# PV with V as weights for column units, and softmax sums added on Pool and VectorE

## The chip, the core and the metric

The kernel runs on one core of a Trainium2 chip. A core has five engines, each with a queue that is worked off in order: PE (TensorE, the matrix multiplier), DVE (VectorE), ACT (ScalarE), POOL (GpSimd) and SP, which here only issues DMA transfers. They share an on-chip memory (SBUF, 128 partitions); PE writes into PSUM, whose banks hold 128 x 512 fp32 values, and DVE and ACT read results from there. Engines wait for each other by semaphores.

The metric is the device time of one execution in microseconds (us). Before the change it is 1303.84 us, the median of three runs (1303.82 to 1304.23).

## What is computed

One transformer block: adaptive layer norm, attention with 32 query heads over 8 cached key and value heads, and a gated MLP. The change concerns the attention:

```python
q = (x @ wq).reshape(B, Sq, Hq, Dh).transpose(0, 2, 1, 3)   # Sq = 2048, Hq = 32, Dh = 128
k = jnp.repeat(k_cache, 4, axis=1)                          # 8 key heads, Sk = 2048
v = jnp.repeat(v_cache, 4, axis=1)
scores = jnp.einsum('bhqd,bhkd->bhqk', q, k) * Dh ** (-0.5)
p = softmax(scores, axis=-1)
o = jnp.einsum('bhqk,bhkd->bhqd', p, v)
return o.transpose(0, 2, 1, 3).reshape(B, Sq, Hq * Dh) @ wo
```

The kernel takes the exponential P of the scaled scores without subtracting a maximum, multiplies it with V, and divides by the sum of P over the keys at the end. (Another path, not taken here, redoes everything if a sum leaves a safe range.)

## The kernel before

**Units.** The attention is cut into 8 x 16 = 128 units: a unit `u` is one key head g = u // 16 and one tile of 128 queries j = u % 16, with the four query heads (REP = 4) that share the key head. A loop over iterations `it` runs 128 units and six more; each iteration has eight slots (NSLOT = 8). In iteration `it`, `qk(it, i)` makes the scores of unit `it` in slot i, and in the same slot PE works off an eighth of the PV product of an earlier unit, a q projection matmul of a coming unit (`fill`), and a matmul of the projection by wo of a still earlier unit. The program order is written out by hand: what stands in a slot is issued there, and `at(it, slot, fn)` puts a function at the head of a slot, behind those put there earlier.

**Two forms of unit.** The scores can be made with the keys on the partitions or with the queries on them.

- A column unit (L1056 to L1070) makes scores transposed: 128 keys of one key tile on the partitions, 512 columns (four heads of 128 queries), two key tiles to a slot. ACT writes their exponential straight to `pTs[u]`, 16 key tiles of 128 x 512, which is the form that PV needs. Its PV (`pv`, L1106) takes P as the weights and V as the moving operand: 64 matmuls of 129 columns. The 129th column of V is ones, so the sum of P over the keys comes with it. DVE then takes the reciprocal (L1125) and normalises into `onorms[u]` (L1126), a DMA transpose turns this to `oTs[u]` (L1137), and the four matmuls by wo (L1171) are added up in one PSUM bank, which DVE adds to `xaccs[j]` (L1158).
- A row unit (L1017 to L1037) has queries on the partitions and 1024 keys to a slot. ACT sums each row while it takes the exponential (`accum_out`), so the sums cost nothing more than two small DVE operations (L1082, L1085), and a DMA transpose (L1078, one for each head) turns P into `pTs[u]`. Its PV (`pv_rows`, L1087) takes V as the weights and P as the moving operand: 16 matmuls of 512 columns, whose result is already transposed; DVE copies it to `oTs[u]` (L1102). As nothing is normalised yet, each head's wo matmul gets a bank of its own, and DVE scales it by the reciprocal sum while adding (L1164).

From unit 5 to 121 the forms come in threes, row, row, column: `by_rows(u)` tells which. 78 units are row units. Units 7, 10, ..., 109 and 112, 115, 118, 121 are the column units among them. PV of a row unit runs two or three iterations after its scores (`LAGS`), PV of a column unit in the next iteration; wo comes three iterations after PV. So in a period of three iterations, called C, N1 and N2 in the prediction, C makes the scores of a column unit, N1 runs its PV while it makes the scores of a row unit, and N2 is a second row unit.

**What is shared.** The PSUM name `misc` has two banks, used in turn by the q projection (one head in each iteration, four matmuls in slots 0 to 3, copied to `qT` by DVE, L970, at the end of slot 3) and by the wo matmuls (slots 4 to 7). `s_ps` has two double banks for scores, `o_ps` two banks for PV. P lives in three buffers (`homes`). SP's queue carries all row turns, the turns of `onorms`, and the loads of each head group (L721 to L744); for each new v, Pool sets its column of ones first (L727).

**The last head group** (units 112 to 127) is followed by a second layer norm for each query tile: Pool multiplies and adds 128 x 512 values there (L1187, L1188). DVE normalises (`xn2`), and DMA turns it (`xnT2`), in `ln2`.

Of the kernel before, what the change touches and what calls it, by code (L numbers as in the profile page):

```python
# [10 lines left out]
BF16 = mybir.dt.bfloat16  # L11
FP32 = mybir.dt.float32
ACT = mybir.ActivationFunctionType
ALU = mybir.AluOpType
AX = mybir.AxisListType
P = 128
# [559 lines left out]
def kernel(  # L576
# [19 lines left out]
    nc = tc.nc  # L596
    _, S, D = A_x.shape
    _, HKV, SK, DH = A_k_cache.shape
    HQ = A_wq.shape[1] // DH
    REP = HQ // HKV  # L600
# [4 lines left out]
    NT = S // P  # L605
    NDT = D // P
    NKT = SK // P
# [5 lines left out]
    NSLOT = NKT // 2  # L613
# [26 lines left out]
    res = fast.enter_context(tc.tile_pool(name="res", bufs=1))  # L640
    stat = fast.enter_context(tc.tile_pool(name="stat", bufs=2))
# [3 lines left out]
    late = free_b.enter_context(tc.tile_pool(name="late", bufs=2, side="right"))  # L645
# [27 lines left out]
    def bank2():  # L673
        return psum.tile([P, 1024], FP32, name="s_ps")
# [11 lines left out]
    def normalise(dst, src, mv, rstd):  # L686
        nc.vector.tensor_scalar(
            out=dst,
            in0=src,
            scalar1=mv,  # L690
            scalar2=rstd,
            op0=ALU.subtract,
            op1=ALU.mult,
        )
# [287 lines left out]
    def by_rows(u):  # L982
        return TURN_A <= u < TURN_B and (u - TURN_A) % len(LAGS) < len(LAGS) - 1

    row_units = [u for u in range(NU) if by_rows(u)]

    def pv_at(u):
# [15 lines left out]
    def at(it, slot, fn):  # L1003
        later.setdefault((it, slot), []).append(fn)

    def qk(u, i):
        g, j = divmod(u, NT)
        b, jj = g * NCH + j // CT, j % CT
        if i == 0:
            if homes[u] == "wsp":  # L1010
                pTs[u] = wspp.tile([P, NT, 512], BF16, name="wsp")
            else:
                pTs[u] = late.tile([P, NKT, 512], BF16, name=homes[u], bufs=1)
            if by_rows(u):
                rsums[u] = stat.tile([P, NSLOT], FP32, name="rs")
        s_ps = bank2()
        if by_rows(u):  # L1017
            hh, half = divmod(i, 2)
            for c in range(2):
                k0 = (2 * half + c) * 512  # L1020
                nc.tensor.matmul(  # L1021
                    s_ps[:, c * 512 : (c + 1) * 512],
                    lhsT=qTs[b][:, hh, jj * P : (jj + 1) * P],
                    rhs=groups[g]["kT"][:, k0 : k0 + 512],
                    start=True,
                    stop=True,
                )
            nc.scalar.activation(  # L1028
                out=rows_of(u, hh)[:, half * HK : (half + 1) * HK],
                in_=s_ps[:],  # L1030
                func=ACT.Exp,
                scale=inv_sqrt_dh,
                accum_out=rsums[u][:, i : i + 1],
            )
            if half == 1:
                at(*divmod(u * NSLOT + i + 1, NSLOT), lambda: turn_rows(u, hh))
            return  # L1037
        if u < 2:
            pair, k0 = i // 4, i % 4 * 4
            qs = slice(pair * 256, (pair + 1) * 256)  # L1040
            for kt in range(4):
                nc.tensor.matmul(  # L1042
                    s_ps[:, kt * 256 : (kt + 1) * 256].rearrange("p (r q) -> p r q", r=2),
                    lhsT=groups[g]["kT"][:, (k0 + kt) * P : (k0 + kt + 1) * P],
                    rhs=qTs[b][:, 2 * pair : 2 * pair + 2, jj * P : (jj + 1) * P],
                    start=(kt % 2 == 0),
                    stop=(kt % 2 == 1),
                )
            nc.scalar.activation(
                out=pTs[u][:, k0 : k0 + 4, qs],  # L1050
                in_=s_ps[:].rearrange("p (k q) -> p k q", k=4),
                func=ACT.Exp,
                scale=inv_sqrt_dh,
            )
            return
        for h in range(2):  # L1056
            kt = 2 * i + h
            nc.tensor.matmul(  # L1058
                s_ps[:, h * 512 : (h + 1) * 512].rearrange("p (r q) -> p r q", r=REP),
                lhsT=groups[g]["kT"][:, kt * P : (kt + 1) * P],  # L1060
                rhs=qTs[b][:, :, jj * P : (jj + 1) * P],
                start=True,
                stop=True,
            )
        nc.scalar.activation(  # L1065
            out=pTs[u][:, 2 * i : 2 * i + 2, :],
            in_=s_ps[:].rearrange("p (k q) -> p k q", k=2),
            func=ACT.Exp,
            scale=inv_sqrt_dh,
        )  # L1070

    def rows_of(u, hh):
        return pn[(row_units.index(u) * REP + hh) % len(pn)][:, 0:SK]
# [71 lines left out]

    def wo_proj(u):
        g, j = divmod(u, NT)
        each = by_rows(u)
        ps = {}

        def into(first, X_ps, scale):
            if first:
                xaccs[j] = late.tile([P, D], FP32, name=f"xacc{j}", bufs=1)
            xa = xaccs[j]
            if scale is None and first:
                nc.vector.tensor_copy(out=xa[:], in_=X_ps[:])
            elif scale is None:
                nc.vector.tensor_tensor(out=xa[:], in0=X_ps[:], in1=xa[:], op=ALU.add)  # L1158
            elif first:
                nc.vector.tensor_scalar(  # L1160
                    out=xa[:], in0=X_ps[:], scalar1=scale, scalar2=None, op0=ALU.mult
                )
            else:
                nc.vector.scalar_tensor_tensor(  # L1164
                    out=xa[:], in0=X_ps[:], scalar=scale, in1=xa[:], op0=ALU.mult, op1=ALU.add
                )

        def mm(hh):
            if hh == 0 or each:
                ps[0] = bank("misc")  # L1170
            nc.tensor.matmul(  # L1171
                ps[0][:],
                lhsT=oTs[u][:, hh, :],
                rhs=groups[g]["wo"][:, hh, :],
                start=(hh == 0 or each),
                stop=(hh == REP - 1 or each),
            )
            if each:
                c0 = u * REP + hh
                into(g == 0 and hh == 0, ps[0], rall[:, c0 : c0 + 1])  # L1180
            elif hh == REP - 1:
                into(g == 0, ps[0], None)
            if hh < REP - 1 or g < HKV - 1:
                return
            xa = xaccs[j]
            engine = nc.gpsimd if j < NT - CT else nc.vector
            engine.tensor_tensor(out=xa[:], in0=xa[:], in1=ga_rows[:], op=ALU.mult)  # L1187
            engine.tensor_tensor(  # L1188
                out=x_sb[:, j, :], in0=xa[:], in1=x_sb[:, j, :], op=ALU.add
            )  # L1190
            if j >= NT - CT:
                ln_stats(mv2, j, x_sb[:, j, :])

        return [lambda hh=hh: mm(hh) for hh in range(REP)]

    def ln2(it, j):

        st = {}

        def first():  # L1200
            if j < NT - CT:
                ln_stats(mv2, j, x_sb[:, j, :])
            st["rstd"] = rstd_of(mv2[:, j : j + 1, :], 1, "ln2")

        def second():
            xn = res.tile([P, D], BF16, name="xn2", bufs=2)
            normalise(xn[:], x_sb[:, j, :], mv2[:, j, 0:1], st["rstd"][:, 0:1])
            st["xnT"] = res.tile([P, NDT, P], BF16, name="xnT2", bufs=2)
            nc.sync.dma_start_transpose(out=st["xnT"][:], in_=xn[:])

        def third():
            ch, c0 = j // CT, (j % CT) * P
            if ch not in h2Ts:
                h2Ts[ch] = res.tile([P, NDT, 512], BF16, name="hT", bufs=NCH)
            for dt in range(NDT):
                nc.vector.tensor_scalar(
                    out=h2Ts[ch][:, dt, c0 : c0 + P],
                    in0=st["xnT"][:, dt, :],
                    scalar1=modc[:, 4 * NDT + dt : 4 * NDT + dt + 1],
                    scalar2=modc[:, 3 * NDT + dt : 3 * NDT + dt + 1],  # L1220
                    op0=ALU.mult,
                    op1=ALU.add,
                )

        at(it + 1, 0 if j >= NT - CT else 2, first)
        at(it + 1, 4, second)
        at(it + 2, 3, third)

# [43 lines left out]
        first[j] = ln1_stats(j, 1)  # L1272

    def tile_norm(j):
        xn = res.tile([P, D], BF16, name="xn2", bufs=2)
        normalise(xn[:], x_sb[:, j, :], mv1[:, j, 0:1], first[j][:, 0:1])
        first[j] = xn

# [193 lines left out]
        at(NU + 5, 5 + ch, lambda ch=ch: z2_norm(ch))  # L1472

    def pv_part(u, i, n):
        if by_rows(u):
            return pv_rows(u, i, n)
        for k in range(NSLOT // n):
            pv(u, i * (NSLOT // n) + k)
# [250 lines left out]
```

## Time and profile before

| what | value |
|---|---|
| profiled execution | 1303.83 us, of it span 1302.0 us |
| PE busy | 1287.0 us, 99% of the span |
| ACT busy | 1112.8 us, 85% |
| DVE busy | 685.7 us, 53% |
| POOL busy | 59.0 us, 5% |
| queue that carries SP's transfers | its packets take 87.5% of the time of 16 DMA engines |
| matmuls of PV in column form (L1114) | 3200 |
| matmuls of PV in row form (L1093) | 1248 in all (as weight loads of L1093) |
| granted PE clock | full in every slice |

Busy time is the time in which an instruction of the engine runs, by the hardware profiler. PE's matmuls overlap, so the mean duration of one (379 ns for 512 columns) is longer than the distance from one to the next (0.22 us). In a timeline a line gives the start, the duration, the engine, the line of the kernel, the operation, its output and input tiles, and at its end, in brackets, how long the engine had stood idle and what released it. A window's line gives, for each engine, the busy time in the window and the number of instructions that start in it.

### The profile page before, as it was taken

How to read it: one execution, taken by the hardware profiler on the slowest of the kernel's cores; microseconds unless marked ns; L12 is line 12 of the kernel's file. 1: busy time of each engine (PE TensorE's matmuls, PEld its weight loads, DVE VectorE, ACT ScalarE, POOL GpSimd, SP SyncE). 2: the span in 40 equal slices, each digit the busy share in tenths (PEclk: the TensorE clock that was granted, in tenths of full speed). 3: DMA queues.
4: the chain of work that ended last, by engine and by line, in shares of the span. 5: the costliest groups of instructions: out<-in, count | busy, mean ns of one | idle time of the engine just before them, and what ended most of it. 6: DMA issues, size and time to landing. Idle time of an engine off the chain costs nothing.

```text
span 1302.0 us, 22572 instructions
## 1 busy us (share of the span) xinstructions
PE 1287.0 (99%) x8512; PEld 700.2 (54%) x8665; DVE 685.7 (53%) x1777; ACT 1112.8 (85%) x1683; POOL 59.0 (5%) x99
## 2 busy tenths in 40 slices
PE   9999999999999999999999999999999999999998
PEld 7655555555555555555555555555555556644445
DVE  7545455545554555455545554555455566784444
ACT  7999999999999999999999999999999998650000
POOL 2000000000000000000000000000000133410000
PEclk9999999999999999999999999999999999999999
DMA  7999999999999999999999999999999973254300
GB/s 207 183 188 181 168 184 191 190 166 188 189 181 177 186 174 189 183 171 188 190 175 181 187 192 181 169 195 173 176 193 165 172 146 91 49 138 98 81 21 32
DMA packets 774997, 211.18 MB, mean 162 GB/s; under 512 B 759264, under 2 KB 773216, under 8 KB 774880
## 3 DMA queue, kind: packets, MB, share of 16 engines
q1 hardware_dynamic: 772864, 207.94, 87.5%
q10 hardware_dynamic: 2016, 1.71, 0.4%
q8 instruction: 70, 1.15, 0.4%
q14 instruction: 47, 0.39, 0.1%
HBM read 21.37 MB, written 2.10 MB: 18 GB/s over the span
## 4 chain that ended last, share of the span: by engine, by line
PE 98%; issue 1%; ACT 1%; DMA 0%; SPq 0%; DVE 0%; ACTq 0%
PE s_ps L1021 21%; PE o_ps L1093 20%; PE o_ps L1114 14%; PE s_ps L1058 13%; PE misc L1171 8%; PE misc L959 8%; PE misc L1573 7%; PE s_ps L1397 2%; PE s_ps L1436 2%; PE o_ps L1606 1%; PE s_ps L1042 0%; PE s_ps L1606 0%; DMA kT<-in_A_k_cache_dram 0%; ACT pn L1028 0%; ACT win_sb L1028 0%
## 5 line engine op out<-in xcount | busy, mean ns | idle before, releaser
L1021 PE MATMUL s_ps<-kT,qT 128*128 128x512 bf16 x1219 | 365.0, 379 | 2.3
L1028 ACT ACTIVATE win_sb<-s_ps 128x1024 bf16<-128x1024 f32 x312 | 319.0, 1023 | 3.4 <-PE s_ps L1021 0.7
L1093 PE MATMUL o_ps<-pT,v 128*128 128x512 bf16 x909 | 272.6, 379 | 1.5
L1164 DVE SCALAR_TENSOR_TENSOR xacc<-misc,rall,xacc 128x512 f32<-128x512 f32 x304 | 227.5, 748 | 69.2 <-PE misc L1171 61.7
L1058 PE MATMUL s_ps<-qT,kT 128*128 128x512 bf16 x768 | 228.4, 379 | 0.8
L1065 ACT ACTIVATE pT<-s_ps 128x1024 bf16<-128x1024 f32 x208 | 209.8, 1024 | 11.8 <-PE s_ps L1058 3.6
L1028 ACT ACTIVATE pn<-s_ps 128x1024 bf16<-128x1024 f32 x208 | 212.7, 1023 | 2.3 <-PE s_ps L1021 0.7
L1093 PEld LDWEIGHTS <-v 128*128 128x128 bf16 x1248 | 121.9, 98 | 147.9 <-issue 1.1
L1065 ACT ACTIVATE wsp<-s_ps 128x1024 bf16<-128x1024 f32 x176 | 179.8, 1023 | 12.4 <-PE s_ps L1058 4.6
L1171 PE MATMUL misc<-wo_g,oT 128*128 128x512 bf16 x479 | 181.6, 379 | 1.0
L1021 PEld LDWEIGHTS <-qT 128*128 128x128 bf16 x1248 | 121.4, 98 | 109.4 <-issue 0.4
L959 PE MATMUL misc<-hT,wq_g 128*128 128x512 bf16 (+1 forms) x499 | 178.3, 369 | 0.5
L970 DVE CAST qT<-misc 128x512 bf16<-128x512 f32 x126 | 86.5, 687 | 153.5 <-PE misc L959 153.5
L1114 PEld LDWEIGHTS <-pT 128*128 128x128 bf16 x1792 | 119.6, 98 | 48.8
L1082 DVE TENSOR_TENSOR tot<-rs 128x1 f32<-128x1 f32 x312 | 48.4, 155 | 171.3 <-ACT win_sb L1028 114.9
L1114 PE MATMUL o_ps<-v,pT 128*128 128x129 bf16 x1792 | 137.5, 220 | 0.6
L1058 PEld LDWEIGHTS <-kT 128*128 128x128 bf16 x768 | 74.1, 98 | 81.1 <-issue 1.1
L1114 PEld LDWEIGHTS <-wsp 128*128 128x128 bf16 x1408 | 94.3, 98 | 41.5
L1114 PE MATMUL o_ps<-v,wsp 128*128 128x129 bf16 x1408 | 108.5, 220 | 0.5
L1028 ACT ACTIVATE wmod_a<-s_ps 128x1024 bf16<-128x1024 f32 x104 | 106.3, 1023 | 0.6 <-PE s_ps L1021 0.4
L1573 PE MATMUL misc<-wsp,z 128*128 128x512 bf16 (+2 forms) x554 | 100.1, 336 | 0.3
L1093 PE MATMUL o_ps<-wsp,v 128*128 128x512 bf16 x292 | 87.8, 379 | 0.4
(118 smaller groups left out, 894.6 us busy)
## 6 DMA issues: line engine op xcount, KB each, us to landing
wo_g<-in_A_wo_dram SPq DMA_DIRECT2D x8, 512.0 KB, 4.5
wq_g<-in_A_wq_dram SPq DMA_DIRECT2D x7, 512.0 KB, 4.1
v<-in_A_v_cache_dram SPq DMA_DIRECT2D x7, 512.0 KB, 4.7
wsp<-in_w_mod_dram SPq DMA_DIRECT2D x1, 2048.0 KB, 9.1
pT<-win_sb SPq DMA_TRANSPOSE x117, 5.0
win_sb<-in_B_w_in_dram SPq DMA_DIRECT2D x1, 1792.0 KB, 7.3
x_sb<-in_A_x_dram SPq DMA_DIRECT2D x3, 512.0 KB, 7.0
out_dram<-yout ACTq DMA_DIRECT2D x12, 128.0 KB, 1.7
```

Source lines behind the costliest of these rows:

```text
L959: nc.tensor.matmul(ps[0][:, o0 : o0 + n], lhsT=wqs[g][:, dt, hh * DH : (hh + 1) * DH], rhs=hTs[ch][:, dt, c0 : c0 + n], start=(dt == 0), s ...
L970: nc.vector.tensor_copy(out=dst, in_=src)
L1021: nc.tensor.matmul(s_ps[:, c * 512 : (c + 1) * 512], lhsT=qTs[b][:, hh, jj * P : (jj + 1) * P], rhs=groups[g]["kT"][:, k0 : k0 + 512], sta ...
L1028: nc.scalar.activation(out=rows_of(u, hh)[:, half * HK : (half + 1) * HK], in_=s_ps[:], func=ACT.Exp, scale=inv_sqrt_dh, accum_out=rsums[u ...
L1058: nc.tensor.matmul(s_ps[:, h * 512 : (h + 1) * 512].rearrange("p (r q) -> p r q", r=REP), lhsT=groups[g]["kT"][:, kt * P : (kt + 1) * P], ...
L1065: nc.scalar.activation(out=pTs[u][:, 2 * i : 2 * i + 2, :], in_=s_ps[:].rearrange("p (k q) -> p k q", k=2), func=ACT.Exp, scale=inv_sqrt_dh,)
L1082: nc.vector.tensor_tensor(out=tot[:], in0=rs[:, 2 * hh : 2 * hh + 1], in1=rs[:, 2 * hh + 1 : 2 * hh + 2], op=ALU.add)
L1093: nc.tensor.matmul(o_pss[u][:], lhsT=groups[g]["v1"][:, kt, 0:DH], rhs=pTs[u][:, kt, :], start=(kt == 0), stop=(kt == NKT - 1),)
L1114: nc.tensor.matmul(o_ps[:, hh % 2, 0 : DH + 1], lhsT=pTs[u][:, kt, hh * P : (hh + 1) * P], rhs=groups[g]["v1"][:, kt, 0 : DH + 1], start=( ...
L1164: nc.vector.scalar_tensor_tensor(out=xa[:], in0=X_ps[:], scalar=scale, in1=xa[:], op0=ALU.mult, op1=ALU.add)
L1171: nc.tensor.matmul(ps[0][:], lhsT=oTs[u][:, hh, :], rhs=groups[g]["wo"][:, hh, :], start=(hh == 0 or each), stop=(hh == REP - 1 or each),)
L1573: nc.tensor.matmul(g_pss[f][:, :n], lhsT=z2[:, st, f * P : (f + 1) * P], rhs=wsp[t][:, st, c0 : c0 + n], start=(st == 0), stop=(st == NT - ...
```

## The change

`by_sums(u)` names the column units among the row units that lie before the last head group: 35 units, 7, 10, ..., 109. They keep their scores (column form), but:

- PV takes V as the weights (`pv_rows`): 16 matmuls of 512 columns instead of 64 of 129. The ones column no longer gives the sums.
- `key_sums(u)` makes the sums. Pool adds key tiles 0 to 11 into an fp32 tile, eleven adds of 128 x 512, put into the slots of iteration u. DVE adds key tiles 12 to 15 into another, three adds, at slots 0, 1 and 2 of iteration u + 1. At slot 4 of u + 1 Pool joins the two into a bf16 tile. This holds, for each of 128 keys modulo the tile, a partial sum for 512 columns. At slot 0 of u + 2 SP issues a DMA transpose that puts queries on the partitions, and at slot 1 of u + 3 DVE sums over the 128 values that are left for each head and takes the reciprocal.
- The wo projection takes the form of a row unit: four banks, four scaled adds.

The fp32 tiles `acc` take the room of `xn2` and `xnT2`; `ln2` uses the two halves of one `acc` tile in their place, and the first tiles' normalisation a half of one.

```diff
+    def by_sums(u):
+        return TURN_A <= u < (HKV - 1) * NT and not by_rows(u)
...
             if by_rows(u):
                 rsums[u] = stat.tile([P, NSLOT], FP32, name="rs")
+            if by_sums(u):
+                key_sums(u)
...
+    N_POOL = 12
+
+    def key_sums(u):
+        acc = [res.tile([P, D], FP32, name="acc", bufs=2) for _ in range(2)]
+        pT = pTs[u]
+
+        def add(engine, a, kt, first):
+            engine.tensor_tensor(
+                out=a[:],
+                in0=pT[:, first, :] if kt == first + 1 else a[:],
+                in1=pT[:, kt, :],
+                op=ALU.add,
+            )
+
+        for kt in range(1, N_POOL):
+            at(*divmod(u * NSLOT + kt // 2 + 1, NSLOT), lambda kt=kt: add(nc.gpsimd, acc[0], kt, 0))
+        for kt, (unit, slot) in zip(range(N_POOL + 1, NKT), ((1, 0), (1, 1), (1, 2))):
+            at(u + unit, slot, lambda kt=kt: add(nc.vector, acc[1], kt, N_POOL))
+
+        def join():
+            onorms[u] = late.tile([P, REP, P], BF16, name="onorm", bufs=3)
+            nc.gpsimd.tensor_tensor(
+                out=onorms[u][:],
+                in0=acc[0][:].rearrange("p (r q) -> p r q", r=REP),
+                in1=acc[1][:].rearrange("p (r q) -> p r q", r=REP),
+                op=ALU.add,
+            )
+
+        turned = {}
+
+        def turn():
+            xn = res.tile([P, D], BF16, name="xn1", bufs=4)
+            turned["t"] = xn[:].rearrange("p (r q) -> p r q", r=REP)
+            nc.sync.dma_start_transpose(
+                out=turned["t"], in_=onorms[u][:].rearrange("p r q -> p (r q)")
+            )
+
+        def close():
+            tot = stat.tile([P, REP], FP32, name="tot4")
+            nc.vector.tensor_reduce(out=tot[:], in_=turned["t"], axis=AX.X, op=ALU.add)
+            nc.vector.reciprocal(out=rall[:, u * REP : (u + 1) * REP], in_=tot[:])
+
+        at(u + 1, 4, join)
+        at(u + 2, 0, turn)
+        at(u + 3, 1, close)
...
     def wo_proj(u):
         g, j = divmod(u, NT)
-        each = by_rows(u)
+        each = by_rows(u) or by_sums(u)
...
-            xn = res.tile([P, D], BF16, name="xn2", bufs=2)
-            normalise(xn[:], x_sb[:, j, :], mv2[:, j, 0:1], st["rstd"][:, 0:1])
-            st["xnT"] = res.tile([P, NDT, P], BF16, name="xnT2", bufs=2)
-            nc.sync.dma_start_transpose(out=st["xnT"][:], in_=xn[:])
+            both = res.tile([P, D], FP32, name="acc", bufs=2)[:].bitcast(BF16)
+            xn = both[:, 0:D]
+            normalise(xn, x_sb[:, j, :], mv2[:, j, 0:1], st["rstd"][:, 0:1])
+            st["xnT"] = both[:, D : 2 * D].rearrange("p (d q) -> p d q", d=NDT)
+            nc.sync.dma_start_transpose(out=st["xnT"], in_=xn)
...
     def pv_part(u, i, n):
-        if by_rows(u):
+        if by_rows(u) or by_sums(u):
             return pv_rows(u, i, n)
```

## The prediction

> **What bounds the kernel now.** I read the page first: the engine totals and the chain of waits.
>
> ```profile
> PE 1287.0 (99%) x8512; PEld 700.2 (54%) x8665; DVE 685.7 (53%) x1777; ACT 1112.8 (85%) x1683; POOL 59.0 (5%) x99
> PE 98%; issue 1%; ACT 1%; DMA 0%; SPq 0%; DVE 0%; ACTq 0%
> ```
>
> The chain is PE from end to end, so an edit changes the time by what it does to PE's stream: work in it, or a stall of it. VectorE (53%) and Pool (5%) cost nothing until PE waits for one of them. Next I cut one period of three units into windows, from one unit's first score matmul to the next one's.
>
> ```profile
> core 0: us, PE busy (x) PEld busy (x) DVE busy (x) ACT busy (x) POOL busy (x), PEclk, DMA share, GB/s
> 561.71:570.34 8.63, 8.58 (x41) 3.91 (x40) 4.52 (x9) 8.24 (x10) 0.00 (x0) 1.00 1.13 190
> 570.34:579.14 8.80, 8.75 (x88) 5.97 (x88) 3.41 (x12) 8.71 (x16) 0.00 (x0) 1.00 0.62 116
> 579.14:587.78 8.64, 8.59 (x41) 3.92 (x40) 5.16 (x16) 8.63 (x17) 0.00 (x0) 1.00 1.09 183
> ```
>
> I call the first window C (a column unit u makes its P), the second N1 (u+1 makes its scores while PV of u runs, 64 matmuls of 129 columns), the third N2. N1 is 0.16 us longer than N2, whose PV is 16 matmuls of 512 columns. No window shows PE waiting.
>
> **What PE gains.** The change gives 35 column units (u = 7, 10, ..., 109) the 512-column PV. N1 then takes N2's 8.64 us: 35 x 0.16 = 5.6 us less, if nothing makes PE wait. The projection by wo keeps its four matmuls per unit; they now take one PSUM bank each.
>
> **What VectorE and Pool get.** These are the rows for the new operations:
>
> ```profile
> L1187 POOL TENSOR_TENSOR xacc<-xacc,ga_rows 128x512 f32<-128x512 f32 x12 | 15.3, 1276 | 215.6 <-DVE xacc L1158 180.4 <-DVE xacc L1164 35.2
> L1188 POOL TENSOR_TENSOR x_sb<-xacc,x_sb 128x512 bf16<-128x512 f32 x12 | 13.8, 1154 | 0.9
> L1187 DVE TENSOR_TENSOR xacc<-xacc,ga_rows 128x512 f32<-128x512 f32 x4 | 2.8, 692 | 0.1
> L1553 DVE TENSOR_REDUCE okm<-tmp 128x1 f32<-128x512 f32 x1 | 0.7, 686 | 0.0
> ```
>
> VectorE loses two reciprocals and two normalisations, 2 x (0.17 + 0.42) = 1.18 us by their rows (L1125, L1126), and one add into xacc (L1158, 0.68). It gets a copy to oT (0.69, as L1102), three adds of P (3 x 0.69), four scaled adds into xacc (L1164, 4 x 0.75), the reduce (0.69) and a reciprocal (0.17): 6.62 us. Net 4.8 us per column unit, 35 x 4.8 = 167 us: 853 of some 1300, a share that alone would not bind. Pool gets 11 adds and the join. An add takes one fp32 and one bf16 input and writes fp32: L1187 has its output type, L1188 its inputs, so it lies between 1.15 and 1.27; I take the middle, 1.21. With the gap of 0.07 between two Pool instructions (below), 11 x 1.28 = 14.1 us, longer than C. So Pool is still adding during most of N1, where VectorE makes its three adds.
>
> **Whether the two can run side by side.** Here the trace speaks, in the last head group, where Pool works beside VectorE:
>
> ```profile
> 1022.84 1.27 POOL L1187 TENSOR_TENSOR xacc<-xacc,ga_rows 128x512 f32<-128x512 f32 x1 [165.43 <-DVE xacc L1158]
> ...
> 1023.73 0.39 DVE L1082 TENSOR_TENSOR tot<-rs 128x1 f32<-128x1 f32 x1
> ...
> 1024.18 1.15 POOL L1188 TENSOR_TENSOR x_sb<-xacc,x_sb 128x512 bf16<-128x512 f32 x1
> 1024.25 0.75 DVE L1164 SCALAR_TENSOR_TENSOR xacc<-misc,rall,xacc 128x512 f32<-128x512 f32 x1
> ...
> 1110.05 0.41 DVE L687 TENSOR_SCALAR xn<-x_sb,mv,rstd_ln 128x512 bf16<-128x512 bf16 x1
> 1110.21 1.37 POOL L1187 TENSOR_TENSOR xacc<-xacc,ga_rows 128x512 f32<-128x512 f32 x1 [1.84 <-DVE xacc L1164]
> ```
>
> The tiny sum of two SBUF columns (L1082, median 0.15) took 0.39 and ended at 1024.12, the moment the Pool operation ended (1024.11). The other two L1082 that fell into an L1187 did the same (0.40 and 0.41). The scaled add, one input in PSUM, took its usual 0.75 beside a Pool operation. So a VectorE operation with two SBUF inputs waits until the Pool operation has ended. The last two lines show Pool waiting: it started under a VectorE operation that ended at 1110.46, and ended 1.12 after that, against 1.27. In both directions about 0.15 of fixed cost hides in the wait. The Trainium skill says this as a rule (SBUF — State Buffer, § Who interferes with whom): a VectorE instruction with two SBUF inputs and a GpSimd instruction that reads SBUF take one port pair by an exclusive lock, held for the whole instruction. The three sums agree. This rule speaks against the change: by it the time rises as below, without it the sum is the gain of 5.6 alone.
>
> All adds of P have both inputs in SBUF, and each add waits for the one before it, so after one VectorE add the waiting Pool operation goes next, and the reverse. That is how I count N1.
>
> **N1 step by step** (us from its start, 570.34 in this trace):
>
> ```profile
> 562.34 8.58 ACT L1065 ACTIVATE pT<-s_ps 128x1024 bf16<-128x1024 f32 x8
> ...
> 570.93 0.74 DVE L1164 SCALAR_TENSOR_TENSOR xacc<-misc,rall,xacc 128x512 f32<-128x512 f32 x1
> ...
> 585.40 0.38 PE L1171 MATMUL misc<-wo_g,oT 128*128 128x512 bf16 x1
> ```
>
> Pool starts when the first exponential of C is done (562.34 + 1.02) plus 0.05, at -6.93. With a pitch of 1.28 its seventh add runs from 0.75 to 1.96. VectorE is held by the last scaled add of C until 570.93 + 0.74, and can start the next 0.08 before that: 1.25. Its first add waits for the seventh Pool add, and needs 0.69 - 0.15 = 0.54, say 0.55, after it: 2.51. A round of one Pool add (1.21 - 0.15 = 1.06) and one VectorE add (0.55) is 1.61: the second add ends at 4.12, the third at 5.73. Then comes the sum L1082 of the row unit, behind the tenth Pool add: 5.73 + 1.06 + 0.02 = 6.81. Behind it are queued its reciprocal and the copy to qT (L970), which ends 0.81 later, and PE sees that 0.05 after: 7.67.
>
> Who waits for the copy? Bank "misc" has two buffers, and an iteration takes five in turn: the q projection, then four for wo. So the second wo matmul needs the bank of the q projection. In N2 it runs at 585.40 - 579.14 = 6.26. PE stands for 1.41 us, then needs N2's remaining 8.64 - 6.26 = 2.38, and about 0.14 at the third wo matmul, since the first scaled add is behind one more L1082 and the last Pool add. N1 becomes 7.67 + 2.38 + 0.14 = 10.19 in place of 8.80: +1.39, times 35 = +49 us. PE's own gain is in this already. In N2 Pool has only the join, VectorE has 3 us free and catches up.
>
> **Bounds of the sum.** Pool add at 1.15: the seventh ends at 1.54, PE is free at 7.07, N1 is 9.54, +26 us. At 1.27: 2.38, 8.27, 10.84, +71. At 1.27 with nothing hidden (1.34 and 0.69 in full) the copy ends at 8.85, N1 is 11.5, +94. For less, see the second rival. The Trainium skill (GPSIMD Engine Reference, § 3.1) gives 4497 ns for 2048 elements; a quarter, 1.12, is an estimate by which it would be +14 us.
>
> **Edits at nothing.** The DMA turn of the sums has the size of the turn of onorm that it replaces. It now stands ahead of the last row turn of u+1 on SP's queue; that one landed at 583.73 and is needed at 587.78, so 4.05 us cover the 1.2 us, and cost 1 us of PE per unit for each us beyond. Pool's own memset for the next v (L727, 0.20) stands ahead of the adds in seven of the column units, which delays Pool by that much there and v not at all. Join: by the count Pool is done at about 9.3, N2 starts at 10.2, so SP doesn't wait for it. The closing reduce comes two iterations before wo needs it. The buffer of P is not written before N2's first turn. In the last head group ln2's two buffers become halves of one: the same number of copies in the same order. Added matmuls: none.
>
> **Rivals.**
> 1. Not slower: after one wait VectorE keeps the port for its three adds (its next one is ready 0.03 after the last, as dependent VectorE operations in this trace follow each other) and Pool waits instead. Then the adds end near 4, L1082 at 4.2, the copy at 5.0 to 5.4, before 6.26; Pool ends later, with its join at about 10, and the 4.05 us cover the turn. Time 1303.8 - 5.6 = 1298. For: nothing shows a fair turn between waiting adds. Against: between dependent adds the port is free for 0.03, and Pool stands waiting. It decides below 2 us of waiting in all.
> 2. Only VectorE waits, Pool's adds are not held up by it: the tenth Pool add ends at 5.80, PE is free at 6.66, N1 is 9.14, +12 us: 1316 (1298 at 1.15, 1335 at 1.27). Against it stands the 1.37 of L1187.
> 3. The change doesn't reach PE's end: ACT is busy 8.71 of N1's 8.80 us; if that holds N1, the gain is nil and the time 1304. Against: N2 runs the same eight exponentials in 8.64.
>
> **How the numbers follow.** The profiled execution is the 1302.0 span plus 1.8 around it, 1303.83, and the median of the runs is 1303.84, so the sum stands against either: 1303.8 + 49 = 1352. Chances: the alternation 0.70 (own range 1328 to 1398), rival 1 0.14, rival 2 0.13 (a fifth of it faster or the same), rival 3 0.03. The one case on the other side lies only 30 us below the likeliest range, and leaving it out with the tails would leave more than 2 in 10 out; so the range is 1297 to 1398. Faster by over 0.2% (what a measurement can tell here): 0.16. Within: 0.03. Slower: 0.81.
>
> **What would show it.** In the profile after: VectorE's adds of P last well over 0.69, about 1.6 each, and end 0.55 after a Pool add ends; Pool's adds lengthen in N1 alone; the copy to qT ends after 7 us of N1; PE's idle time stands before the second wo matmul (line of "misc"), released by VectorE; N1 is 9.5 to 10.9 us, C and N2 stay at 8.6. The theory is wrong if the VectorE adds last 0.69, or if N1 is 8.64. If they wait and PE doesn't, I have the bank that it needs wrong.

## The result, and the profile after

The changed kernel takes 1341.09 us (median of 5 runs, 1340.97 to 1341.35) against 1303.84: a ratio of 1.0284, 95% interval 1.027 to 1.0298. It is 37 us slower. Forecast were 1352 us, with 1328 to 1398 for the likeliest case and 1297 to 1398 over all.

The page's first line of totals and the chain of waits, of the changed kernel:

```profile
span 1339.2 us, 20171 instructions
...
PE 1292.9 (97%) x6860; PEld 627.9 (47%) x6985; DVE 946.6 (71%) x1952; ACT 1112.0 (83%) x1683; POOL 582.0 (43%) x519
...
PE 78%; DVE 20%; issue 1%; ACT 1%; DMA 0%; SPq 0%; DVEq 0%; ACTq 0%
```

Before, the chain was PE for 98% of the span; now VectorE (DVE) holds 20% of it. PE's idle time (span less busy) went from 15.0 to 46.3 us. The waits of PE tell for whom. A line gives who waited, for what, the total in us, how many times, and the longest:

```profile
PE misc L1222 <- DVE qT L970: 30.9, 34, 1.1
```

L1222 is the wo matmul (L1171 before), L970 the copy of the q projection to qT. Nearly every one of the 35 column units has one such wait. Other line numbers have moved too: L1133 is the row unit's small sum (L1082 before), L1215 the scaled add (L1164 before), and L1084 is the helper that makes every add of P, on Pool and on VectorE. `pT` and `wsp` are two of the three buffers of P.

The three windows C, N1 and N2 of a period in the middle (the columns as before: length, then busy time and count for each engine):

```profile
core 0: us, PE busy (x) PEld busy (x) DVE busy (x) ACT busy (x) POOL busy (x), PEclk, DMA share, GB/s
581.19:589.83 8.64, 8.64 (x41) 3.92 (x40) 5.29 (x11) 8.31 (x10) 6.38 (x6) 1.00 0.87 169
589.83:599.73 9.90, 8.90 (x40) 3.90 (x40) 9.55 (x15) 8.64 (x16) 8.57 (x7) 1.00 0.65 123
599.73:608.36 8.63, 8.58 (x40) 3.92 (x40) 5.65 (x16) 8.62 (x17) 0.00 (x0) 1.00 1.10 192
```

C and N2 are as they were. N1 went from 8.80 to 9.90: 1.10 us, times 35 is 38.5 us, some 1 us more than the measured loss of 37. In N1 VectorE shows busy for 9.55 us, but that holds waiting. Its second and third add take 1.49 us each in the mean, where such an add takes 0.69 alone:

```profile
L1084 DVE TENSOR_TENSOR acc<-acc,wsp 128x512 f32<-128x512 f32 x36 | 53.7, 1493 | 2.5
```

The timeline of N1 of the same kernel (start, duration) shows for what they wait:

```profile
590.45 1.15 POOL L1084 TENSOR_TENSOR acc<-acc,pT 128x512 f32<-128x512 f32 x1
591.08 1.07 DVE L1084 TENSOR_TENSOR acc<-pT 128x512 f32<-128x512 bf16 x1
591.68 1.48 POOL L1084 TENSOR_TENSOR acc<-acc,pT 128x512 f32<-128x512 f32 x1
592.26 1.46 DVE L1084 TENSOR_TENSOR acc<-acc,pT 128x512 f32<-128x512 f32 x1
593.25 1.48 POOL L1084 TENSOR_TENSOR acc<-acc,pT 128x512 f32<-128x512 f32 x1
593.75 1.53 DVE L1084 TENSOR_TENSOR acc<-acc,pT 128x512 f32<-128x512 f32 x1
594.81 1.48 POOL L1084 TENSOR_TENSOR acc<-acc,pT 128x512 f32<-128x512 f32 x1
595.20 1.11 DVE L1133 TENSOR_TENSOR tot<-rs 128x1 f32<-128x1 f32 x1
...
596.42 0.67 DVE L970 CAST qT<-misc 128x512 bf16<-128x512 f32 x1
597.01 0.53 DVE L1133 TENSOR_TENSOR tot<-rs 128x1 f32<-128x1 f32 x1
597.15 0.38 PE L1222 MATMUL misc<-wo_g,oT 128*128 128x512 bf16 x1 [0.89 <-DVE qT L970]
...
598.44 0.38 PE L1222 MATMUL misc<-wo_g,oT 128*128 128x512 bf16 x1
```

Read the ends, start plus duration. Pool's add ends at 591.60, VectorE's at 592.15, Pool's at 593.16, VectorE's at 593.72, Pool's at 594.73, VectorE's at 595.28, Pool's at 596.29, and the tiny sum at 596.31. They end one after the other, as if only one of them advanced at a time: after a Pool add VectorE needs 0.55, after a VectorE add Pool needs 1.01. The copy to qT, behind all of that in VectorE's queue, ends at 597.09, and PE's second wo matmul starts 0.06 later. It is then 7.32 us into N1, where N2 of the kernel before has it at 6.26: 1.06 us late. The third wo matmul comes 1.29 after it, in place of 1.08, and loses 0.21 more. The list of waits has only 0.89 of this, since it counts from the end of the matmul before, and matmuls overlap.

### The profile page after: what moved, and what is told of

It is laid out like the page before. It is cut to its first block, busy times and chain, and to the rows that moved or that the text cites. A ratio compares the mean times of both kernels' runs of the same rounds, so it can differ in the third digit from the quotient of the medians.

```text
span 1339.2 us, 20171 instructions
## 1 busy us (share of the span) xinstructions
PE 1292.9 (97%) x6860; PEld 627.9 (47%) x6985; DVE 946.6 (71%) x1952; ACT 1112.0 (83%) x1683; POOL 582.0 (43%) x519
## 4 chain that ended last, share of the span: by engine, by line
PE 78%; DVE 20%; issue 1%; ACT 1%; DMA 0%; SPq 0%; DVEq 0%; ACTq 0%
PE o_ps L1144 21%; PE s_ps L1026 13%; PE s_ps L1063 13%; DVE acc L1084 10%; PE misc L1222 7%; PE misc L1625 7%; PE misc L959 6%; PE o_ps L1165 4%; DVE tot L1133 4%; DVE xacc L1215 3%; PE s_ps L1449 2%; PE s_ps L1488 2%; DVE qT L970 1%; PE o_ps L1658 1%; DVE rall L1136 1%
## 5 line engine op out<-in xcount | busy, mean ns | idle before, releaser
L1215 DVE SCALAR_TENSOR_TENSOR xacc<-misc,rall,xacc 128x512 f32<-128x512 f32 x441 | 328.9, 746 | 71.8 <-PE misc L1222 60.7
L1144 PE MATMUL o_ps<-pT,v 128*128 128x512 bf16 x1157 | 348.2, 379 | 3.1
L1144 PEld LDWEIGHTS <-v 128*128 128x128 bf16 x1808 | 176.8, 98 | 213.4
L1084 POOL TENSOR_TENSOR acc<-acc,wsp 128x512 f32<-128x512 f32 x180 | 225.7, 1254 | 14.1
L1222 PE MATMUL misc<-wo_g,oT 128*128 128x512 bf16 x500 | 189.3, 379 | 32.9 <-DVE qT L970 30.9
L1084 POOL TENSOR_TENSOR acc<-acc,pT 128x512 f32<-128x512 f32 x170 | 213.1, 1254 | 13.3
L959 PE MATMUL misc<-hT,wq_g 128*128 128x512 bf16 (+1 forms) x523 | 187.4, 369 | 0.2
L970 DVE CAST qT<-misc 128x512 bf16<-128x512 f32 x126 | 86.3, 685 | 125.9 <-PE misc L959 125.9
L1144 PE MATMUL o_ps<-wsp,v 128*128 128x512 bf16 x563 | 169.8, 379 | 1.5
L1133 DVE TENSOR_TENSOR tot<-rs 128x1 f32<-128x1 f32 x312 | 95.8, 307 | 47.6 <-ACT win_sb L1033 32.7
L1084 POOL TENSOR_TENSOR acc<-wsp 128x512 f32<-128x512 bf16 x18 | 20.7, 1149 | 216.2 <-ACT wsp L1070 216.2
L1084 POOL TENSOR_TENSOR acc<-pT 128x512 f32<-128x512 bf16 x17 | 19.5, 1149 | 191.2 <-ACT pT L1070 191.2
```

The costliest lines, as they stand in the source:

```text
L959: nc.tensor.matmul(ps[0][:, o0 : o0 + n], lhsT=wqs[g][:, dt, hh * DH : (hh + 1) * DH], rhs=hTs[ch][:, dt, c0 : c0 + n], start=(dt == 0), s ...
L970: nc.vector.tensor_copy(out=dst, in_=src)
L1084: engine.tensor_tensor(out=a[:], in0=pT[:, first, :] if kt == first + 1 else a[:], in1=pT[:, kt, :], op=ALU.add,)
L1133: nc.vector.tensor_tensor(out=tot[:], in0=rs[:, 2 * hh : 2 * hh + 1], in1=rs[:, 2 * hh + 1 : 2 * hh + 2], op=ALU.add)
L1144: nc.tensor.matmul(o_pss[u][:], lhsT=groups[g]["v1"][:, kt, 0:DH], rhs=pTs[u][:, kt, :], start=(kt == 0), stop=(kt == NKT - 1),)
L1215: nc.vector.scalar_tensor_tensor(out=xa[:], in0=X_ps[:], scalar=scale, in1=xa[:], op0=ALU.mult, op1=ALU.add)
```

## The experiments

The theory: adds of P on the two engines alternate on what they read SBUF through (called "the port"; the runs show that the adds take turns, not by which part of the chip); what stands behind VectorE's adds in its queue is late, and PE waits for the PSUM bank that this frees. The main rival, "load": VectorE simply has too much work in N1. Ratios are against the kernel before, run on the same chip (1303.9 us), with 95% intervals.

### Ten of Pool's adds left out

```diff
-        for kt in range(1, N_POOL):
+        for kt in range(1, 2):
```

> Left out: ten of Pool's eleven adds in each column unit, so the sums lack key tiles 2 to 11; VectorE's work is unchanged. Theory (VectorE's adds alternate with Pool's on one port, and the copy to qT behind them keeps PE from the bank of the second wo matmul): no Pool add is left in N1, VectorE's adds fall from 1.07 and 1.49 us to 0.69, the copy to qT ends before 6.2 us of N1, N1 is 8.64 in place of 9.90, and the time is 1303.8 - 5.6 = 1298 us. Rival 'load' (VectorE has too much work in N1, whoever else runs): N1 stays near 9.9 and the time within 5 us of 1341.

Measured: 1297.89 us, ratio 0.9951 (0.9934 to 0.9967). VectorE's rows, with the count, total and mean ns:

```profile
L1084 DVE TENSOR_TENSOR acc<-acc,wsp 128x512 f32<-128x512 f32 x36 | 24.9, 692 | 2.5
L1084 DVE TENSOR_TENSOR acc<-acc,pT 128x512 f32<-128x512 f32 x34 | 23.5, 692 | 2.4
```

The same adds take 692 ns in place of 1493, and no wait of PE for the copy is left in its list. VectorE does all its added work, so its load alone isn't the cause.

### One add moved from VectorE to Pool

```diff
-    N_POOL = 12
+    N_POOL = 13
```

> Pool adds key tiles 0 to 12, VectorE 13 to 15: one add moves from VectorE to Pool. Theory: one round of 1.49 us less before the copy to qT, which then ends at 7.26 - 1.49 = 5.77 us of N1, before the 6.26 at which the second wo matmul is due; N1 is 8.64 to 8.75, time 1298 to 1302 us. Rival 'load': the add is worth its own 0.69 us, of the 1.26 us that N1 is above 8.64 some 0.57 stay, time 1298 + 35 x 0.57 = 1318 us.

Measured: 1298.83 us, ratio 0.9957 (0.994 to 0.9974). The two adds that stay still wait (the second one lasts 1528 ns in the mean), but one round less is enough. In the N1 that starts at 515.76 the copy ends at 5.72 us, where 5.77 was expected, the second wo matmul runs at 6.26, when due, and N1 is 8.63. An add of 0.69 us taken away brought 42 us, 1.2 us per unit; the rival's 1318 is 19 us off.

```profile
L1084 DVE TENSOR_TENSOR acc<-acc,wsp 128x512 f32<-128x512 f32 x18 | 27.5, 1528 | 0.6
...
L1222 PE MATMUL misc<-wo_g,oT 128*128 128x512 bf16 x500 | 189.5, 379 | 0.3
```

In the second line, of PE's wo matmul, the last figure is PE's idle time before it in us: 0.3, where the changed kernel has 32.9.

### VectorE first, Pool after

```diff
-        for kt in range(1, N_POOL):
-            at(*divmod(u * NSLOT + kt // 2 + 1, NSLOT), lambda kt=kt: add(nc.gpsimd, acc[0], kt, 0))
-        for kt, (unit, slot) in zip(range(N_POOL + 1, NKT), ((1, 0), (1, 1), (1, 2))):
-            at(u + unit, slot, lambda kt=kt: add(nc.vector, acc[1], kt, N_POOL))
+        for kt in range(1, 4):
+            at(u, kt // 2 + 2, lambda kt=kt: add(nc.vector, acc[1], kt, 0))
+        for kt in range(5, NKT):
+            at(*divmod(u * NSLOT + kt // 2 + 1, NSLOT), lambda kt=kt: add(nc.gpsimd, acc[0], kt, 4))
...
-        at(u + 1, 4, join)
-        at(u + 2, 0, turn)
+        at(u + 2, 0, join)
+        at(u + 2, 3, turn)
```

> VectorE adds the first four key tiles, early in C and before Pool starts; Pool adds the other twelve, until the end of N1; join, turn and closing follow in N2 and after. Same adds on both engines as in the changed kernel. Theory: only the small sums of the row units wait for Pool in N1 (up to 1.2 us each, only one of them ahead of the copy to qT), so the copy ends before 6.2 us; C, N1 and N2 are 8.63 to 8.75, time 1298 to 1301 us, faster than both kernels. Rival 'load', taken over the period: VectorE's work is the same, 1335 to 1341 us. Rival 'late turn' (the sums' turn, here 1.5 us later than in the changed kernel, holds up the row turns): slower than 1341.

Measured: 1300.32 us, ratio 0.9975 (0.9962 to 0.9988). As many adds on each engine as in the changed kernel, at another time, are faster than the kernel before by 3.6 us (one of six runs, 1303.79, is not). VectorE's last add still meets Pool's first in most units, but there Pool waits (its first add takes 1.56 us in the median, 1.15 alone), and PE needs nothing of Pool's. The run is some 2.5 us slower than the variants at 1297.6 to 1297.9. Most of that is named in the waits:

```profile
DVE tot L1116 <- DMA xn<-onorm: 2.3, 4, 1.3
...
PE misc L1222 <- DVE qT L970: 1.7, 2, 1.5
```

Four times the turn of the sums landed late, and VectorE waited for it in the closing reduce. In two of the four (the reduces at 94.64 and 873.02) VectorE's adds came that much later and met Pool's, and PE waited as in the changed kernel (1.52 and 0.20 us). So there is something in "late turn", but for 1.7 us in all. PE's idle time in this profile is 2.0 us longer than in the next experiment's (15.3 against 13.3); the remaining half us is in PE's busy time, and its cause stays open.

### All adds on Pool

```diff
-        for kt in range(1, N_POOL):
+        for kt in range(1, NKT):
             at(*divmod(u * NSLOT + kt // 2 + 1, NSLOT), lambda kt=kt: add(nc.gpsimd, acc[0], kt, 0))
...
-                out=a[:],
+                out=onorms[u][:].rearrange("p r q -> p (r q)") if kt == NKT - 1 else a[:],
...
-        at(u + 1, 4, join)
-        at(u + 2, 0, turn)
+        at(u + 2, 3, turn)
```

(VectorE's adds and the join are gone.)

> Pool makes all fifteen adds, the last straight to the bf16 tile, so that VectorE has none and no join is needed; the turn is issued at slot 3 of N2. Theory: Pool is busy from 1.65 us of C for 15 x 1.22 = 18.3 us, to 2.7 us of N2; the row units' small sums wait for it, at most 1.2 us each, one of them ahead of the copy to qT, which ends before 6.2 us: time 1298 to 1301 us. Rival 'load': VectorE has 2.1 us less than in the changed kernel, more than the 1.26 that N1 is too long, so also 1298. Rival 'late turn': slower than 1341, since the turn comes some 3 us later.

Measured: 1297.73 us, ratio 0.9949 (0.9933 to 0.9966): it computes all that the changed kernel does and is the fastest of the versions that leave nothing out. It takes 43 us off the changed kernel and 6 off the one before. It doesn't tell the theory from "load", since it takes work from VectorE; the runs above and below do. It does speak against "late turn": seven times VectorE waited for the turn of the sums, 5.3 us in all, and PE never waited for VectorE because of it.

### The adds behind the copy

```diff
-        for kt, (unit, slot) in zip(range(N_POOL + 1, NKT), ((1, 0), (1, 1), (1, 2))):
+        for kt, (unit, slot) in zip(range(N_POOL + 1, NKT), ((1, 4), (1, 4), (1, 4))):
```

> The changed kernel with VectorE's three adds moved from slots 0 to 2 to slot 4 of N1, behind the copy to qT and ahead of the four scaled adds; all else, the work of each engine too, as in the changed kernel. Theory (what stands behind the adds in VectorE's queue is late, and PE waits for the bank that it frees): the copy ends at about 5.2 us and the second wo matmul runs when due; the first add waits for Pool's tenth (5.4), the second for its eleventh (7.0), the third ends at 8.2, so the first scaled add ends at 9.2 and the third wo matmul, due at 7.34, waits for it: PE's idle time moves there, N1 is 10.5, time 1298 + 35 x 1.9 = 1364 us. Rival 'load' (only the amount counts): 1341. Rival 'copy alone' (with the copy out of the way PE is free): 1298.

Measured: 1364.71 us, ratio 1.0464 (1.0446 to 1.0481). PE's waits, and one of them in the timeline:

```profile
PE misc L1222 <- DVE xacc L1215: 55.8, 31, 2.0
PE misc L1222 <- DVE xacc L1211: 5.5, 3, 1.9
```

```profile
523.21 0.69 DVE L970 CAST qT<-misc 128x512 bf16<-128x512 f32 x1 [1.28 <-PE misc L959]
523.81 0.92 DVE L1084 TENSOR_TENSOR acc<-wsp 128x512 f32<-128x512 bf16 x1
524.77 2.25 DVE L1084 TENSOR_TENSOR acc<-acc,wsp 128x512 f32<-128x512 f32 x2
...
527.99 0.38 PE L1222 MATMUL misc<-wo_g,oT 128*128 128x512 bf16 x1 [1.80 <-DVE xacc L1215]
```

The copy is in time, the waits for it are gone, and the scaled adds (L1215 and L1211) have taken its place: 61.3 us in 34 waits, 1.80 each. VectorE's second and third adds wait less than in the changed kernel (they last 1110 ns in the mean against 1493), yet the kernel is 24 us slower. What counts is which operation stands behind them, and how much room that one has.

### Pool busy without reading

```diff
-        for kt in range(1, N_POOL):
-            at(*divmod(u * NSLOT + kt // 2 + 1, NSLOT), lambda kt=kt: add(nc.gpsimd, acc[0], kt, 0))
+        at(u, 1, lambda: add(nc.gpsimd, acc[0], 1, 0))
+        for k in range(N_MEM):                             # 24
+            at(u, 2 + k % 6, lambda: nc.gpsimd.memset(acc[0][:], 1.0))
```

> Ten of Pool's eleven adds are left out (the sums lack key tiles 2 to 11 and are wrong), and 24 memsets of the same 128 x 512 fp32 tile stand in their place, so that Pool is busy beside VectorE but reads nothing. Theory A (the two share what they read SBUF through): VectorE's adds last 0.69 us beside a memset and the time is 1298 us. Theory B (any Pool instruction holds up a VectorE add): an add lasts 0.69 plus up to one memset and the time lies between 1298 and 1341, by how long a memset is. If the memsets end before N1 the run tells nothing.

Measured: 1297.64 us, ratio 0.9952 (0.9935 to 0.9968). The memsets do reach into N1; the timeline around VectorE's adds (in this kernel the adds are L1085, the memsets L1094, the small sum L1135):

```profile
516.15 2.85 POOL L1094 MEMSET acc<- 128x512 f32 x5
516.56 0.68 DVE L1085 TENSOR_TENSOR acc<-pT 128x512 f32<-128x512 bf16 x1
517.34 1.42 DVE L1085 TENSOR_TENSOR acc<-acc,pT 128x512 f32<-128x512 f32 x2
518.68 0.15 DVE L1135 TENSOR_TENSOR tot<-rs 128x1 f32<-128x1 f32 x1
```

Five memsets run back to back from 516.15 to 519.00, and VectorE's three adds and the tiny sum, all within them, take 0.68, 0.69, 0.69 and 0.15 us, as long as alone. So it isn't Pool being busy that holds VectorE up; what Pool's adds have and its memsets lack is that they read SBUF. Theory A holds. The Trainium skill states the same (SBUF — State Buffer, § Who interferes with whom): a VectorE instruction with two SBUF inputs contends with a GpSimd instruction that reads SBUF, not with one that only writes it.

## Why the prediction was right

The likeliest case came true with its mechanism, place and order; the size was 49 us forecast against 37 measured. The range over all, 1297 to 1398, tells little by itself, since it holds the times of all three rivals too (1298, 1316 and 1304); what bears the forecast out is the sequence of steps. Step by step, in us from the start of N1 (589.83):

| step | forecast | measured |
|---|---|---|
| Pool's seventh add ends | 1.96 | 1.77 |
| VectorE's adds end | 2.51, 4.12, 5.73 | 2.32, 3.89, 5.45 |
| sum of the row unit ends | 6.81 | 6.48 |
| copy to qT ends | 7.62 | 7.26 |
| second wo matmul starts | 7.67 | 7.32 |
| length of N1 | 10.19 | 9.90 |

- **The bank.** The second wo matmul, the copy behind the adds, and the two buffers of "misc" were named rightly. Putting the adds behind the copy moved PE's wait to the bank that the theory says, by 1.80 us where 1.9 was expected.
- **The alternation.** After each wait VectorE needs 0.55 us and Pool 1.01, where 0.55 and 1.06 were taken; the 0.05 are Pool's add itself (next point). That Pool would wait for an add of VectorE rested on one row, the 1.37, and the VectorE operation there was a tensor_scalar (L687) with one tensor as input, not an add of two. That it holds for adds was a guess, which the 1.48 of Pool's adds bear out.
- **The mis-sized term** is Pool's add. I put it in the middle of two rows, 1.21; it takes 1.157 (median), the row with one bf16 input. At the bound for 1.15 the forecast had N1 at 9.54, too short, since Pool started at -6.77, not -6.93. The two errors partly cancel. Put into the same steps, 1.157 and -6.77 give 7.30 for the second wo matmul and 9.82 for N1. Of the 0.29 us by which N1 was forecast too long, 0.19 stand already in the end of the seventh add, 0.16 more came from there to the second wo matmul (the three rounds, 0.14 of it), and the third wo matmul, late by 0.21 in place of 0.14, gave 0.07 back.
- **The upper bound** was added up too short. With 1.34 and 0.69 in full the steps give 2.38 + 3 x 2.03 + 0.02 + 0.81 = 9.30 for the copy, not 8.85, and so about 1413 in place of 1398. The fixed cost was hidden as forecast, so nothing came of it.
- **PE's gain.** Forecast 5.6 us; of the variants in which PE doesn't wait for VectorE's copy, three (1297.64, 1297.73, 1297.89) are 6.0 to 6.3 us below the kernel before, and the one with one add moved (1298.83) is 5.1 below.
- **Rival 1**, VectorE keeping the port, fell: each engine gets one instruction, then the other one. **Rival 2**, Pool not held up, fell: Pool's adds between VectorE's last 1.48. **Rival 3**, ACT holding N1, fell: the same exponentials fit into a total 6 us shorter.
- **Edits at nothing.** The join ended at 598.87, before N2 (599.73) in which SP issued the turn, as counted. Where the turn was moved later VectorE waited for it, 2.3 us in the third experiment and 5.3 in the fourth; only in the third did that reach PE.

VectorE's forecast work of 853 us can be read where hardly anything waits: 841.9 us with ten of Pool's adds left out. VectorE runs the same instructions in both, so the 946.6 of the changed kernel hold 105 us of waiting.

## What to carry to other kernels

Two adds on two engines that both read SBUF took turns here: 1.56 us for the pair, 0.3 less than their two durations alone (0.69 + 1.157). Who pays is whatever stands behind the waiting one in its queue. So before work goes to an idle engine, ask what it reads beside, and whether the next instruction in the waiting engine's queue frees something the bound engine needs. Where the first engine has time for all of it, as Pool had here, splitting the work can be what costs; and moving the waiting work by a few slots can cure the stall or make it worse.

## What the runs showed that was not expected

- The cost of a Pool add follows its inputs, not its output. In the version with all adds on Pool (mean ns), fp32 and bf16 inputs take the same to an fp32 tile as to a bf16 tile, and the join of two fp32 tiles in the changed kernel, to bf16, takes 1271 ns. L1187 before, a product of two fp32 inputs to an fp32 tile, has 1267 in the median. All have 128 x 512 values:

```profile
L1086 POOL TENSOR_TENSOR acc<-acc,pT 128x512 f32<-128x512 f32 x221 | 255.5, 1156 | 17.3
...
L1086 POOL TENSOR_TENSOR onorm<-acc,pT 128x512 bf16<-128x512 f32 x17 | 19.6, 1153 | 1.3
```

- VectorE's closing reduce, with one SBUF input, ran beside a Pool add (582.72 to 583.39, Pool from 583.06) and neither was longer: 0.67 and 1.15 us.
- A busy share can hide a wait: VectorE at 71% looked as if it had work, and a ninth of it (105 of 946.6 us) was standing at a port.
